# Thresholded attention and a leaky MLP on one core: q rows of two heads interleaved over the partitions, and the k and q loads placed earlier

## The chip, the cores and the metric

The kernel runs on one core of a Trainium2 chip. A core has TensorE (matrix products; in the profile PE for the products and PEld for the loads of their stationary operand, LDWEIGHTS), VectorE (DVE), ScalarE (ACT), GpSimd (POOL) and SyncE (SP), which run their own instruction streams and wait for each other on semaphores, and 16 DMA engines. The metric is device time in microseconds of one execution; smaller is better.

## The reference

Eight batches, eight heads, 576 tokens, head size 64. Attention keeps only scores within tau = 0.02 of their row's largest; then a two-layer MLP with a leaky ReLU runs over the concatenated heads.

```python
scores = scale * np.matmul(q, k.transpose(0, 1, 3, 2))          # scale = 1/8
thresh = np.max(scores, axis=-1, keepdims=True) - tau
scores = np.where(scores >= thresh, scores, -1e9)
scores = scores - np.max(scores, axis=-1, keepdims=True)
attn = np.exp(scores)
attn = attn / (np.sum(attn, axis=-1, keepdims=True) + 1e-09)
x = np.matmul(attn, v)                      # heads are then put side by side: (4608, 512)
h = x @ w_in                                # (512, 2048)
out = np.maximum(0.01 * h, h) @ w_out       # (2048, 512)
```

## The kernel before

**Steps.** The work is cut into 144 steps, 18 for each batch. The 576 rows of a batch are held as 64 partitions of nine consecutive tokens, so a block of 128 query rows is two of the nine token places t for 64 partitions each; the ninth place of two head pairs makes a block together. The heads are taken in four pairs p; a pair is the heads h = 0 and h = 1 of `(h f)`, that is f and f + 4. A step is one block of queries of one pair: two score tiles `sc[0]`, `sc[1]` of 128 queries x 576 keys. The steps of one block pair and one head pair (or, for the ninth place, two steps over all four pairs) make a unit; in the last batch some units are one step long.

**Number format.** q and k are float32. Each is split, scaled by 64, into a float16 high part and a float16 remainder (`hi` on ScalarE, L149; `x64` and `lo` on GpSimd, L153 and L159; in batch 0 `lo` on VectorE, L160). A score is the sum of three float16 products, high x high, high x low and low x high (`PRODS`).

**Halves and transposes.** A batch's q and k come in two halves hb, each with two head pairs g = 0, 1. `load_half` (L96) brings a half as a tile `km` or `qm` of 128 partitions, partition 64 f + p, where f is the pair within the half and p the row group. After the split, `ks` and `qs` hold (part, t, head, d) per partition. TensorE needs them with (head, d) on the partitions, so they are transposed. For k, one DMA transpose on SP (`turn`, L175) takes the whole 128-partition tile: 18 blocks of 128 x 128. For q, two DMA transposes (L179), one for each pair g, take 64 partitions each and write to `qst[:, g]`, so that the weights of a score product, `qt[r, g, qi, ds(2 * c, 2), :]`, are 128 neighbouring columns. In batch 0 alone TensorE does these transposes (`turn_pe`), and PSUM is copied out by ScalarE (L197) or VectorE (L199).

**One step.** Scores on TensorE (`scores`, L338, and L344 for the ninth place); eviction with row maximum on VectorE (`smax`, L398); the shift by maximum and tau, on ScalarE for one head (L524) and GpSimd for the other (L523, L525); one step later the clipping on VectorE (L554) and the exponentials with row sums on ScalarE (L559). Two steps after a unit's last step the reciprocals of its sums are put beside its weights in `w` (L542, L544), and a DMA transpose on SP turns `w` into `wt` (L548). Five steps after that, `LAG` = 7 after the last step, TensorE multiplies with v (`pv`, L369), VectorE scales into `xT` (L379, L385), and MLP units follow: `hp` and `op` products (L243), Relu on ScalarE (L257), the leak on VectorE (L223), eviction (L279), and the output's DMA on SP (L280).

**Order.** The program is laid out by hand in the loop over steps s, and every engine and queue runs its own instructions in that order. At the end of a step the functions listed for it in `ptick` and then `tick` are emitted. For half hb of batch b, with s0 = 18 (b - 1) and t0 = s0 + PREP[hb], PREP = (3, 9), (4, 9) for b = 1:

- k is loaded at step t0 - 4 and q at t0 - 3;
- `hi` of k runs on ScalarE at t0 - 1, of q at t0 + 1;
- `x64` and `lo` run on GpSimd at t0 to t0 + 6;
- k is transposed at t0 + 4, q's two pairs at t0 + 7 and t0 + 8.

So within a batch's 18 steps, the next batch's half 0 has `hi` at 2 and 4 and transposes at 7, 10 and 11; half 1 has `hi` at 8 and 10, transposes at 13, 16 and 17. The loads for half 1 stand at 5 and 6, those for half 0 at 17 of the batch before and 0. Weight transposes stand at the odd steps. All plain loads of q and k, all DMA transposes and all output stores are issued by SP, in order; v, w_in and w_out come by GpSimd's queue. `km`, `qm`, `ks` and `qs` have two buffers each, `kst` and `qst` four, `wt` four.

Of the kernel before, what the change touches and what calls it, by code (L numbers as in the profile page):

```python
# [10 lines left out]
FP16 = mybir.dt.float16  # L11
# [5 lines left out]
def kernel(  # L17
# [22 lines left out]
    nc = tc.nc  # L40
# [18 lines left out]
    ENDS = 130  # L59
    WOUT = 0  # L60
    SPOOL = 5

    sb = ctx.enter_context(tc.tile_pool(name="sb", bufs=1))
    ps = ctx.enter_context(tc.tile_pool(name="ps", bufs=1, space=bass.MemoryType.PSUM))
# [6 lines left out]
    if tau_f > 1.0:  # L71
# [10 lines left out]
        out=ident, in_=ident, compare_op=AX.is_equal, fill=0.0, base=0, pattern=[[-1, 128]], channel_multiplier=1)  # L82
# [6 lines left out]
    qms, kms, vts, qsts, ksts = {}, {}, {}, {}, {}  # L89
    qss, kss = {}, {}  # L90

    def load_half(src, store, nm, b, hb):


        m = store[b, hb] = sb.tile([128, 2, 576], FP32, tag=nm, bufs=2, name=nm)
        nc.sync.dma_start(  # L96
            out=m, in_=src[b, :, :, :].rearrange("(h f) (p t) d -> f p h (t d)", h=2, t=9)[
                ds(2 * hb, 2)].rearrange("f p h x -> (f p) h x"))

    anchor = [None]  # L100

# [25 lines left out]
    def split_tile(nm, b, hb):  # L127
        store = kss if nm == "k" else qss
        if (b, hb) not in store:
            store[b, hb] = sb.tile([128, 2, 9, 2, 64], FP16, tag=nm + "s", bufs=2, name=nm + "s")  # L130
        return store[b, hb]
# [31 lines left out]
    def turned(nm, b, hb):  # L163

        store = ksts if nm == "k" else qsts
        if (b, hb) not in store:
            shape = [128, 2, 9, 2, 64] if nm == "k" else [128, 2, 2, 9, 64]
            store[b, hb] = sb.tile(shape, FP16, tag=nm + "st", bufs=4, name=nm + "st")
        return store[b, hb]

    def turn(nm, b, hb, g=None):
        t = turned(nm, b, hb)
        s_ = split_tile(nm, b, hb)
        if nm == "k":
            nc.sync.dma_start(  # L175
                out=t.rearrange("p s t g r -> p (s t) (g r)"), in_=s_.rearrange("p s t h d -> p (s t h d)"),
                transpose=True)
        else:
            nc.sync.dma_start(  # L179
                out=t[:, g].rearrange("p s t r -> p (s t) r"),  # L180
                in_=s_[ds(64 * g, 64)].rearrange("p s t h d -> p (s t h d)"), transpose=True)

    def turn_pe(nm, b, hb, i, pieces, eng):

        t = turned(nm, b, hb)
        s_ = split_tile(nm, b, hb)
        for t0, n, tag, bufs, w in pieces:
            p_ = ps.tile([128, w, 128], FP16, tag=tag, bufs=bufs, name="tp")
            for j in range(n):
                nc.tensor.transpose(p_[:, j, :], s_[:, i, t0 + j, :, :].rearrange("p h d -> p (h d)"), ident)  # L190
            if nm == "k":
                src, dst = p_[:, 0:n, :], t[:, i, ds(t0, n), :, :].rearrange("p t g r -> p t (g r)")
            else:
                src = p_[:, 0:n, :].rearrange("p t (g r) -> p g t r", g=2)
                dst = t[:, :, i, ds(t0, n), :]
            if eng == "act":
                nc.scalar.activation(out=dst, in_=src, func=AF.Copy, bias=0.0, scale=1.0)  # L197
            else:
                nc.vector.tensor_copy(out=dst, in_=src)  # L199
# [125 lines left out]
    def scores(s, sc):  # L325

        b, c, p = steps[s]
        for t0, n in ((0, 5), (5, 4)):
            cols = ds(SC0 + 64 * t0, 64 * n)
            for i, (qi, ki) in enumerate(PRODS):  # L330
                for u in range(1 if c < 4 else 2):
                    hb, g = divmod(p + u, 2)
                    for h in range(2):
                        r = ds(64 * h, 64)
                        rhs = ksts[b, hb][r, ki, ds(t0, n), g, :]
                        qt = qsts[b, hb]
                        if c < 4:
                            nc.tensor.matmul(  # L338
                                out=sc[h][:, cols],
                                lhsT=qt[r, g, qi, ds(2 * c, 2), :].rearrange("p t r -> p (t r)"),  # L340
                                rhs=rhs, start=(i == 0), stop=(i == 2),
                                skip_group_check=True, tile_position=(64 * h, 0))
                        else:
                            nc.tensor.matmul(  # L344
                                out=sc[h][ds(64 * u, 64), cols], lhsT=qt[r, g, qi, 8, :],
                                rhs=rhs, start=(i == 0), stop=(i == 2),
                                skip_group_check=True, tile_position=(64 * h, 64 * u))

# [56 lines left out]
    def at(s, f, t=tick):  # L405
        t.setdefault(max(0, s), []).append(f)
# [55 lines left out]
    for b in range(1, B):  # L462
        s0 = 18 * (b - 1)
        for hb in range(2):
            t0 = s0 + (PREP1 if b < 2 else PREP)[hb]
            at(t0 - 4, lambda b=b, hb=hb: load_half(k, kms, "km", b, hb))
            at(t0 - 3, lambda b=b, hb=hb: load_half(q, qms, "qm", b, hb))
            at(t0 - 1, lambda b=b, hb=hb: hi("k", b, hb))
            at(t0 + 1, lambda b=b, hb=hb: hi("q", b, hb))

            for i, what in enumerate(("k0x", "k0l", "k1x q0x", "k1l", "q0l", "q1x", "q1l")):
                for w in what.split():
                    nm, h = w[0], int(w[1])
                    if w[2] == "x":
                        at(t0 + i, lambda nm=nm, h=h, b=b, hb=hb: after_anchor(x64(nm, b, hb, h)), ptick)
                    else:
                        for part in PARTS[nm]:
                            at(t0 + i, lambda nm=nm, h=h, b=b, hb=hb, part=part: after_anchor(lo(nm, b, hb, h, part)), ptick)
            at(t0 + 4, lambda b=b, hb=hb: turn("k", b, hb))
            for g in range(2):  # L480
                at(t0 + 7 + g, lambda b=b, hb=hb, g=g: turn("q", b, hb, g))
        for i in range(4):
            at(18 * b + i, lambda b=b, i=i: load_v(b, i))

# [12 lines left out]
    for s in range(NS + LAG + 1):  # L497
# [7 lines left out]
        while credit >= 1.0:  # L505
            f = next_o()
            if f:
                ou.append(f)
            f = next_h()
# [4 lines left out]
        if live:  # L514
            sc = [ps.tile([128, 1024], FP32, tag=f"sc{h}", bufs=1, name=f"sc{h}") for h in range(2)]
            scores(s, sc)
        last, prev = prev, None
        if live:
# [7 lines left out]
                out=P_[:, 0, :], in0=sa, scalar1=1.0, scalar2=bb[:, 0:1], op0=AX.mult, op1=AX.add)  # L526
            prev = (P_,) + unit_of[s]
        leak()
        for i in range(max(len(ou), len(hu))):
            o = ou[i]() if i < len(ou) else None  # L530
            h = hu[i]() if i < len(hu) else None
# [7 lines left out]
        if now is not None:  # L539
# [5 lines left out]
                out=W_[:, :, 1152:1280].rearrange("p i (h r) -> p i h r", h=2),  # L545
# [3 lines left out]
                out=uwt[now][:, 0:nw].rearrange("p i j r -> p (i j) r"), in_=W_.rearrange("p i c -> p (i c)"),  # L549
                transpose=True)  # L550
        if last is not None:
            P_, ui, i = last
# [22 lines left out]
    while hq or oq or leaky:  # L575
        for nx in (next_o, next_h):
            leak()
            f = nx()
            if f:
                f = f()  # L580
# [39 lines left out]
```

## Time and profile before

| | |
|---|---|
| median of 6 runs | 537.36 us (536.32 to 538.35) |
| the profiled execution | 536.81 us, of it 535.1 us from the first to the last instruction |
| granted TensorE clock, mean | 0.949 |
| DVE sf (L398), 288 | 746 ns each |
| LDWEIGHTS of scores, 64x128 (L338), 1536 | 97 ns each |
| score products of 320 columns, 768 | 313 ns each |
| LDWEIGHTS of v, 128x64 (L369), 1000 | 111 ns each |
| wt transposes on SP, 76 | 3.68 us median to issue, 6.1 us to land |
| kst transposes, 14 | 43.4 us of issue in all, 5.4 us to land |
| qst transposes, 28 | 41.8 us of issue in all, 4.3 us to land |
| km, qm loads, 16 each, 576 KB | 5.3 and 6.0 us to land |

How to read it: a page shows one execution. Busy time is per engine. A group of instructions is named by the line of the kernel, the engine, the operation and the tiles (out<-in). SPq is SP's queue of DMA issues: the time shown there is that of issuing, and the landing is told apart. The view of waits names the waiting engine and line, and what it waited for: microseconds in all, times, longest. In the timeline each line is a start and a length in microseconds, then the instruction; idle time before it stands in brackets. DMA share is the mean busy share of the 16 DMA engines; packets overlap, so that it can exceed 1. The chain of waits follows the work that ended last back through whatever released it.

### The profile page before, as it was taken

How to read it: one execution, taken by the hardware profiler on the slowest of the kernel's cores; microseconds unless marked ns; L12 is line 12 of the kernel's file. 1: busy time of each engine (PE TensorE's matmuls, PEld its weight loads, DVE VectorE, ACT ScalarE, POOL GpSimd, SP SyncE). 2: the span in 40 equal slices, each digit the busy share in tenths (PEclk: the TensorE clock that was granted, in tenths of full speed). 3: DMA queues.
4: the chain of work that ended last, by engine and by line, in shares of the span. 5: the costliest groups of instructions: out<-in, count | busy, mean ns of one | idle time of the engine just before them, and what ended most of it. 6: DMA issues, size and time to landing. Idle time of an engine off the chain costs nothing.

```text
span 535.1 us, 13446 instructions
## 1 busy us (share of the span) xinstructions
PE 476.2 (89%) x4912; PEld 294.3 (55%) x4912; DVE 463.2 (87%) x1213; ACT 421.5 (79%) x924; POOL 276.9 (52%) x476
## 2 busy tenths in 40 slices
PE   4657785999989997999989995999999998999996
PEld 3324453556555663666555663566655665566663
DVE  5976896999999996999998995899999999999542
ACT  6785885988799886898888985898799888688331
POOL 5475844675576645584566643575477643222000
PEclk9756897999999997999999998899999999999999
DMA  8999999999999999999999999999999999976401
GB/s 275 203 189 255 161 196 237 225 182 182 228 229 204 163 189 265 225 180 192 214 191 195 181 186 263 229 188 187 207 204 231 185 171 176 190 128 127 95 22 59
DMA packets 279617, 101.79 MB, mean 190 GB/s; under 512 B 254464, under 2 KB 266752, under 8 KB 279552
## 3 DMA queue, kind: packets, MB, share of 16 engines
q1 hardware_dynamic: 266496, 92.03, 90.6%
q0 software_dynamic: 13056, 8.92, 12.2%
q8 instruction: 38, 0.62, 0.5%
q14 instruction: 27, 0.22, 0.1%
HBM read 36.70 MB, written 9.44 MB: 86 GB/s over the span
## 4 chain that ended last, share of the span: by engine, by line
DVE 39%; PE 18%; issue 14%; DMA 13%; POOL 6%; ACT 6%; SPq 3%; POOLq 0%; DVEq 0%; ACTq 0%
DVE sf L398 15%; DMA km<-in_k_dram 8%; DVE gT L223 7%; DVE P L554 7%; PE op L243 6%; PE hp L243 5%; DMA wt<-w 4%; PE sc L338 4%; DVE w L544 4%; POOL P L525 3%; DVE osb L279 3%; DVE xT L379 2%; SPq L179 2%; PE pv L369 2%; ACT P L524 1%
## 5 line engine op out<-in xcount | busy, mean ns | idle before, releaser
L398 DVE TENSOR_SCALAR_CACHE_REDUCE sf<-sc 128x576 f32<-128x576 f32 x288 | 204.9, 746 | 9.9 <-PE sc L338 8.9
L559 ACT ACTIVATE w<-P 128x576 f16<-128x576 f16 x288 | 193.7, 674 | 8.1 <-DVE P L554 3.9
L243 PE MATMUL op<-wout,gT 128*128 128x512 f16 x576 | 151.0, 386 | 12.0 <-DVE osb L279 11.6
L243 PE MATMUL hp<-xT,win 128*128 128x256 f16 (+1 forms) x1344 | 153.9, 261 | 6.5 <-DVE gT L223 4.7
L338 PE MATMUL sc<-kst,qst 64*128 64x320 f16 (+1 forms) x1536 | 137.4, 298 | 19.4 <-DVE sf L398 18.7
L524 ACT ACTIVATE P<-sf,bb 128x576 f16<-128x576 f32 x144 | 111.1, 772 | 45.4 <-POOL bb L523 41.3
L243 PEld LDWEIGHTS <-win 128*128 128x128 f16 x1344 | 118.3, 99 | 51.1 <-issue 10.0
L223 DVE SCALAR_TENSOR_TENSOR gT<-hp,gT 128x512 f16<-128x512 f32 x144 | 98.2, 682 | 32.0 <-ACT gT L257 32.0
L338 PEld LDWEIGHTS <-qst 64*128 64x128 f16 x1536 | 76.2, 97 | 70.6 <-issue 51.9
L525 POOL TENSOR_SCALAR P<-sf,bb 128x576 f16<-128x576 f32 x139 | 104.8, 754 | 14.1
L257 ACT ACTIVATE gT<-hp 128x512 f16<-128x512 f32 x144 | 83.4, 579 | 18.9 <-PE hp L243 18.9
L243 PEld LDWEIGHTS <-gT 128*128 128x128 f16 x576 | 46.5, 98 | 75.2 <-issue 40.4
L523 POOL TENSOR_SCALAR bb<-mx 128x2 f32<-128x2 f32 x139 | 27.2, 196 | 109.5 <-DVE sf L398 99.4
L554 DVE TENSOR_SCALAR P<-P 128x1152 int16<-128x1152 int16 x144 | 81.5, 566 | 0.0
L369 PE MATMUL pv<-wt,v 128*64 128x256 f16 (+2 forms) x1000 | 55.7, 250 | 9.4 <-DMA wt<-w 9.3
L559 ACT ACTIVATION_READ_ACCUMULATOR w<-P 128x1 f32 x288 | 54.3, 188 | 0.0
L369 PEld LDWEIGHTS <-v 128*64 128x64 f16 x1000 | 37.4, 111 | 25.5 <-issue 22.2
L159 POOL TENSOR_TENSOR ks<-km,ks 128x320 f16<-128x320 f32 (+1 forms) x56 | 39.8, 730 | 11.4 <-DVE P L554 10.7
L149 ACT ACTIVATE ks<-km 128x640 f16<-128x640 f32 (+1 forms) x32 | 20.0, 672 | 30.6 <-DMA km<-in_k_dram 30.6
L159 POOL TENSOR_TENSOR qs<-qm,qs 128x576 f16<-128x576 f32 x28 | 35.8, 1279 | 14.2 <-DVE P L554 14.2
L544 DVE TENSOR_SCALAR w<-rc 128x256 f16<-128x256 f32 (+1 forms) x76 | 39.6, 521 | 2.6
L379 DVE TENSOR_TENSOR xT<-pv,wt 128x128 f16<-128x128 f32 x128 | 31.6, 289 | 5.9 <-PE pv L369 5.8
(35 smaller groups left out, 211.4 us busy)
## 6 DMA issues: line engine op xcount, KB each, us to landing
km<-in_k_dram SPq DMA_DIRECT2D x16, 576.0 KB, 5.3
qm<-in_q_dram SPq DMA_DIRECT2D x16, 576.0 KB, 6.0
out_dram<-osb SPq DMA_DIRECT2D x36, 256.0 KB, 3.7
v<-in_v_dram POOLq DMA_DIRECT2D x16, 160.0 KB, 5.6
v<-in_v_dram POOLq DMA_DIRECT2D x16, 128.0 KB, 5.8
win<-in_moe_w_in_dram POOLq DMA_DIRECT2D x8, 256.0 KB, 9.9
wout<-in_moe_w_out_dram POOLq DMA_DIRECT2D x8, 256.0 KB, 11.4
wt<-w SPq DMA_TRANSPOSE x76, 6.1
```

Source lines behind the costliest of these rows:

```text
L159: return nc.gpsimd.tensor_tensor(out=dst[:, h], in0=src[:, h], in1=h_[:, h], op=AX.subtract)
L223: nc.vector.scalar_tensor_tensor(out=G.g[u], in0=hp, scalar=0.01, in1=G.g[u], op0=AX.mult, op1=AX.add)
L243: nc.tensor.matmul(out=out_, lhsT=lhsT, rhs=rhs, start=start, stop=stop, skip_group_check=True)
L257: nc.scalar.activation(out=G.g[u], in_=hp, func=AF.Relu, bias=0.0, scale=0.99)
L338: nc.tensor.matmul(out=sc[h][:, cols], lhsT=qt[r, g, qi, ds(2 * c, 2), :].rearrange("p t r -> p (t r)"), rhs=rhs, start=(i == 0), stop=(i ...
L369: nc.tensor.matmul(out=o_[ds(64 * h, 64)], lhsT=vt[:, pp, h, j, :], rhs=w_[:, :, 4 * h + j, :], start=(j == 0), stop=(j == 4), skip_group_ ...
L398: nc.vector.tensor_scalar(out=sf, in0=sc[h][:, ds(SC0, 576)], scalar1=C, scalar2=None, op0=AX.mult, op1=AX.max, accum_out=mx[:, h : h + 1])
L524: nc.scalar.activation(out=P_[:, 1, :], in_=sB, func=AF.Identity, bias=bb[:, 1:2], scale=1.0)
L525: (nc.vector if s < SPOOL else nc.gpsimd).tensor_scalar(out=P_[:, 0, :], in0=sa, scalar1=1.0, scalar2=bb[:, 0:1], op0=AX.mult, op1=AX.add)
L544: nc.vector.tensor_scalar(out=W_[:, :, 1152:1280].rearrange("p i (h r) -> p i h r", h=2), in0=rc[:, 0:nw, :].unsqueeze(3).to_broadcast([12 ...
L554: anchor[0] = nc.vector.tensor_scalar(out=pi, in0=pi, scalar1=NEG, scalar2=None, op0=AX.max)
L559: nc.scalar.activation(out=uW[ui][:, i, ds(576 * h, 576)], in_=P_[:, h, :], func=AF.Exp, bias=exp_bias, scale=1.0, accum_out=usm[ui][:, i, ...
```

## The change

The q tile is loaded so that the two head pairs of a half take turns on the partitions: partition 2 p + f in place of 64 f + p. This takes two DMAs of 64 partitions each, every second one. `hi`, `x64` and `lo` are untouched, as they work on each partition alone. The transposed q tile then has the same shape as k's, with 128 columns for each part and token place in which the columns of pair g are every second one, and one DMA transpose of 128 partitions (at t0 + 7) stands in place of the two. The score products take their stationary operand at every second column, `[:, g::2]`. In batch 0 the copies out of PSUM write qst in the order in which it lies.

The loads of the next batch are placed by `LOADS = (-4, 3)`: for half 0, k at s0 - 4 and q at s0 - 3; for half 1, k at s0 + 3 and q at s0 + 4. For b = 1 the places of half 0 are below zero and become step 0. `hi`, `x64`, `lo` and the k transposes stay where they were.

```diff
@@ -59,6 +59,7 @@
     ENDS = 130
     WOUT = 0
     SPOOL = 5
+    LOADS = (-4, 3)
 
     sb = ctx.enter_context(tc.tile_pool(name="sb", bufs=1))
     ps = ctx.enter_context(tc.tile_pool(name="ps", bufs=1, space=bass.MemoryType.PSUM))
@@ -92,10 +93,14 @@
     def load_half(src, store, nm, b, hb):
 
 
+
         m = store[b, hb] = sb.tile([128, 2, 576], FP32, tag=nm, bufs=2, name=nm)
-        nc.sync.dma_start(
-            out=m, in_=src[b, :, :, :].rearrange("(h f) (p t) d -> f p h (t d)", h=2, t=9)[
-                ds(2 * hb, 2)].rearrange("f p h x -> (f p) h x"))
+        in_ = src[b, :, :, :].rearrange("(h f) (p t) d -> f p h (t d)", h=2, t=9)[ds(2 * hb, 2)]
+        if nm == "km":
+            nc.sync.dma_start(out=m, in_=in_.rearrange("f p h x -> (f p) h x"))
+        else:
+            for f in range(2):
+                nc.sync.dma_start(out=m.rearrange("(p f) h x -> f p h x", f=2)[f], in_=in_[f])
 
     anchor = [None]
 
@@ -164,21 +169,13 @@
 
         store = ksts if nm == "k" else qsts
         if (b, hb) not in store:
-            shape = [128, 2, 9, 2, 64] if nm == "k" else [128, 2, 2, 9, 64]
-            store[b, hb] = sb.tile(shape, FP16, tag=nm + "st", bufs=4, name=nm + "st")
+            store[b, hb] = sb.tile([128, 2, 9, 2, 64], FP16, tag=nm + "st", bufs=4, name=nm + "st")
         return store[b, hb]
 
-    def turn(nm, b, hb, g=None):
-        t = turned(nm, b, hb)
-        s_ = split_tile(nm, b, hb)
-        if nm == "k":
-            nc.sync.dma_start(
-                out=t.rearrange("p s t g r -> p (s t) (g r)"), in_=s_.rearrange("p s t h d -> p (s t h d)"),
-                transpose=True)
-        else:
-            nc.sync.dma_start(
-                out=t[:, g].rearrange("p s t r -> p (s t) r"),
-                in_=s_[ds(64 * g, 64)].rearrange("p s t h d -> p (s t h d)"), transpose=True)
+    def turn(nm, b, hb):
+        nc.sync.dma_start(
+            out=turned(nm, b, hb).rearrange("p s t g r -> p (s t) (g r)"),
+            in_=split_tile(nm, b, hb).rearrange("p s t h d -> p (s t h d)"), transpose=True)
 
     def turn_pe(nm, b, hb, i, pieces, eng):
 
@@ -188,11 +185,7 @@
             p_ = ps.tile([128, w, 128], FP16, tag=tag, bufs=bufs, name="tp")
             for j in range(n):
                 nc.tensor.transpose(p_[:, j, :], s_[:, i, t0 + j, :, :].rearrange("p h d -> p (h d)"), ident)
-            if nm == "k":
-                src, dst = p_[:, 0:n, :], t[:, i, ds(t0, n), :, :].rearrange("p t g r -> p t (g r)")
-            else:
-                src = p_[:, 0:n, :].rearrange("p t (g r) -> p g t r", g=2)
-                dst = t[:, :, i, ds(t0, n), :]
+            src, dst = p_[:, 0:n, :], t[:, i, ds(t0, n), :, :].rearrange("p t g r -> p t (g r)")
             if eng == "act":
                 nc.scalar.activation(out=dst, in_=src, func=AF.Copy, bias=0.0, scale=1.0)
             else:
@@ -337,12 +330,12 @@
                         if c < 4:
                             nc.tensor.matmul(
                                 out=sc[h][:, cols],
-                                lhsT=qt[r, g, qi, ds(2 * c, 2), :].rearrange("p t r -> p (t r)"),
+                                lhsT=qt[r, qi, ds(2 * c, 2)].rearrange("d t a b -> d (t a b)")[:, g::2],
                                 rhs=rhs, start=(i == 0), stop=(i == 2),
                                 skip_group_check=True, tile_position=(64 * h, 0))
                         else:
                             nc.tensor.matmul(
-                                out=sc[h][ds(64 * u, 64), cols], lhsT=qt[r, g, qi, 8, :],
+                                out=sc[h][ds(64 * u, 64), cols], lhsT=qt[r, qi, 8].rearrange("d a b -> d (a b)")[:, g::2],
                                 rhs=rhs, start=(i == 0), stop=(i == 2),
                                 skip_group_check=True, tile_position=(64 * h, 64 * u))
 
@@ -463,8 +456,8 @@
         s0 = 18 * (b - 1)
         for hb in range(2):
             t0 = s0 + (PREP1 if b < 2 else PREP)[hb]
-            at(t0 - 4, lambda b=b, hb=hb: load_half(k, kms, "km", b, hb))
-            at(t0 - 3, lambda b=b, hb=hb: load_half(q, qms, "qm", b, hb))
+            at(s0 + LOADS[hb], lambda b=b, hb=hb: load_half(k, kms, "km", b, hb))
+            at(s0 + LOADS[hb] + 1, lambda b=b, hb=hb: load_half(q, qms, "qm", b, hb))
             at(t0 - 1, lambda b=b, hb=hb: hi("k", b, hb))
             at(t0 + 1, lambda b=b, hb=hb: hi("q", b, hb))
 
@@ -477,8 +470,7 @@
                         for part in PARTS[nm]:
                             at(t0 + i, lambda nm=nm, h=h, b=b, hb=hb, part=part: after_anchor(lo(nm, b, hb, h, part)), ptick)
             at(t0 + 4, lambda b=b, hb=hb: turn("k", b, hb))
-            for g in range(2):
-                at(t0 + 7 + g, lambda b=b, hb=hb, g=g: turn("q", b, hb, g))
+            at(t0 + 7, lambda b=b, hb=hb: turn("q", b, hb))
         for i in range(4):
             at(18 * b + i, lambda b=b, i=i: load_v(b, i))
```

## The prediction

> **What bounds the kernel now.** I read the page first.
>
> ```profile
> PE 476.2 (89%) x4912; PEld 294.3 (55%) x4912; DVE 463.2 (87%) x1213; ACT 421.5 (79%) x924; POOL 276.9 (52%) x476
> DMA  8999999999999999999999999999999999976401
> ```
>
> TensorE and VectorE are busy for almost nine tenths, and so, in every slice up to the tail, are the DMA engines. Which of them sets the pace is read by stretch. The next view gives busy time from the first score eviction of one batch to that of the next, for batches 1 to 6 (first column: window; then its length, busy time of PE, PEld, DVE, ACT, POOL; the granted clock, the DMA share and GB/s).
>
> ```profile
> 70.40:132.10 61.70, 54.15 (x548) 32.71 (x547) 55.27 (x145) 50.13 (x113) 35.92 (x60) 0.94 1.09 205
> 132.10:189.70 57.60, 54.93 (x602) 34.84 (x601) 56.29 (x148) 51.27 (x115) 35.40 (x60) 1.00 1.13 208
> 189.70:251.80 62.10, 58.24 (x577) 35.00 (x576) 55.96 (x149) 51.36 (x115) 35.47 (x60) 0.95 1.09 207
> 251.80:311.00 59.20, 56.19 (x609) 35.29 (x608) 56.13 (x148) 51.17 (x115) 35.44 (x60) 1.00 1.16 195
> 311.00:374.80 63.80, 58.23 (x577) 35.11 (x576) 55.91 (x149) 51.37 (x115) 35.46 (x60) 0.95 1.13 211
> 374.80:432.50 57.70, 56.38 (x609) 35.47 (x608) 56.28 (x148) 51.26 (x115) 35.40 (x60) 1.00 1.13 207
> ```
>
> The six batches take 362.1 us, 60.35 each, and they alternate: a long one is followed by a short one. VectorE does the same 56 us of work in each. What the engines alone would need: in an undisturbed stretch the chain's sf pieces start at 289.46, 295.65, 301.96, 308.13 and 314.43, 6.24 us for two steps, and one pair of a batch takes 6.8 (404.18 to 410.99); 8 x 6.24 + 6.8 = 56.7 us. So 3.6 us of a batch is loss, 21.9 us over the six. The DMA share is above 1 throughout (packets overlap).
>
> Where the loss shows, from the view of waits:
>
> ```profile
> ACT ks L149 <- DMA km<-in_k_dram: 30.6, 9, 6.3
> PE pv L369 <- DMA wt<-w: 9.3, 5, 4.2
> ```
>
> ScalarE stands still for a k load, most often at step 2 of a batch's own count, and sometimes TensorE for a transposed weight tile. The timeline around 140 us shows why the load is late:
>
> ```profile
> 131.59 1.30 SPq L179 DMA_TRANSPOSE qst<-qs  x1
> 133.07 4.56 SPq L548 DMA_TRANSPOSE wt<-w  x1
> 137.68 1.34 SPq L179 DMA_TRANSPOSE qst<-qs  x1
> 139.07 1.33 SPq L96 DMA_DIRECT2D km<-in_k_dram  x1
> ...
> 141.77 13.77 SPq L548 DMA_TRANSPOSE wt<-w  x3
> 144.56 1.26 ACT L149 ACTIVATE ks<-km 128x640 f16<-128x640 f32 x2 [1.81 <-DMA km<-in_k_dram]
> ```
>
> SP issues without a pause, and behind its work: VectorE had finished the w of the weight transpose at 141.77 by 138.13. Read the same way, the same unit's transpose was 6.2 us late one batch on (195.75 to 201.90), then 2.8, 8.3 and 3.2. The long batches (stalled on k) let SP catch up; in the short ones it falls behind again, by 2.5, 5.5 and 3.4 us. So the in-order SP queue with the DMA engines behind it needs about 60 to 65 us a batch, more than the engines' 56.7: it is the bound in the middle, and the k stall is how that shows.
>
> What makes the queue slow:
>
> ```profile
> qm<-in_q_dram SPq DMA_DIRECT2D x16, 576.0 KB, 6.0
> wt<-w SPq DMA_TRANSPOSE x76, 6.1
> qst<-qs SPq DMA_TRANSPOSE x28, 4.3
> kst<-ks SPq DMA_TRANSPOSE x14, 5.4
> ```
>
> A k transpose of 128 partitions lands in 5.4 us; one of q, of 64 and so half the data, in 4.3. Two stretches with only transpose packets moving, the first a q transpose (issued 131.59), the second a weight transpose (133.07):
>
> ```profile
> 133.00:134.50 1.50, 1.50 (x22) 0.99 (x21) 1.50 (x4) 1.31 (x4) 0.77 (x2) 1.00 0.99 143
> 137.00:138.50 1.50, 1.50 (x16) 0.86 (x15) 1.47 (x5) 1.26 (x2) 0.88 (x2) 1.00 1.27 290
> ```
>
> The last column is the point: 143 GB/s against 290 with no other traffic beside either. The half-height transpose drains at half the rate.
>
> **The change part by part**, against the profiled execution's 536.8 us (span 535.1 and 1.7 around it); the median of six runs is 537.36, 0.6 above.
>
> (a) Two q transposes become one of 128 partitions, 14 times. Each half is 18 x 64 x 256 bytes = 295 KB, 2.06 us at 143 GB/s, 4.12 for two. The whole one is 590 KB: 2.03 us at 290 GB/s if the queue is backed up, 3.10 if it goes as kst's mean issue on SP (43.4 us for 14). Saved per pair 1.0 to 2.1 us; two pairs a batch, 2.0 to 4.2 us; I take the middle, 3.1. SP's own issue time stays: two at 1.49 (41.8 us over 28) against one at 3.10.
>
> (b) k and q loads move on SP: for half 0 of the next batch from steps 17 and 18 to 14 and 15, for half 1 from 5 and 6 to 3 and 4. k of half 0 is thereby issued ahead of one weight transpose (step 15), both q transposes (16, 17) and the weight transpose of 17: in the timeline from 139.07 to about 127, where the k transpose of step 13 ends (issued 123.26, 3.60 long). With 5.5 to 6.4 us to land it is there by about 133, and ScalarE asks at 142.7. For half 1 the lead grows from 9 to 15 us of program steps, against the worst seen, 8 us late plus 6.8 to land. So the k waits in the loop go: 5.7, 1.8, 4.5, 1.4, 6.3 and 1.9 us for half 0, 4.4 and 2.2 for half 1. That time is no gain by itself, since it is what let SP catch up. What is late next is the weight transpose: the one issued behind the moved loads is pushed back by their 0.6 + 2 x 0.47 us of issue and some 3.5 us of transfer (1.18 MB at the 330 GB/s of the load stretch, 142 to 147 us). Its multiplication comes 5 to 8 us after landing where SP keeps up (landed 126.97, used 133.53), 0.04 where it doesn't (446.23, 446.27). In return the weight transpose of step 1, the one with the smallest slack today, has two loads fewer ahead of it. Buffers don't hold the loads: km and qm have two, and the last reader of the earlier use (POOL's L159, step 15 at the latest for half 1, 9 for half 0) comes before both new places.
>
> (c) Each q load becomes two of 64 partitions, every second one: one more issue of 0.47 us, 16 times, 7.5 us of SP time. In the loop SP has that, as its long transposes (wt 3.7 median, 3.0 at best) wait on the drain and not on issue. At the start it lies on the chain (a qm piece from 1.32 us on, 4.91 long): +0.5. The Trainium skill, "DMA: Bandwidth & Descriptors", Rules for kernel authors, speaks against this part: two transfers over parts of the partitions serialize, and one of 128 should be used. Its figure of about 2 us fixed per DMA (Anatomy of one DMA, for the other kind of queue) would add, as an estimate by that page, 28 us over the 14 loop loads if none overlapped; km and qm landing 1.5 us apart here (86.57, 88.05) shows that they do overlap.
>
> (d) The score weights (L338, L344) are read at every second column. No strided weight load is in the trace. Nearest rows: 64x128 at 97 ns, 128x64 at 111 ns: 128 columns load faster than 64, so there is a fast way that a stride may lose. Bounds: 0, and 2 x 111 - 97 = 125 ns more per load. Loads of the two heads run in pairs (12 in 0.63 us beside 12 matmuls in 0.91), so six a step are serial: 0 to 0.75 us a step; a part hides behind matmuls of 120 ns. A gain is excluded, nothing gets narrower. I take 0, by the nearest row in shape (the same 64x128 load), and keep the other end as a rival. On this the skill's "TensorE: Matmul & The Clock Gate", Weight-path perf modes, says that the fast load holds for 128 weights in packed or strided columns up to a step of 1,024, but also that it reads 32 bits at a time, which at every second 16-bit column carries one weight in place of two; no run here shows which tells.
>
> (e) The PSUM copies of batch 0's q (L199, 752 ns) write runs in order; at most 0.3 us, taken as 0.
>
> Sum: a batch needs 60.35 - 3.1 = 57.25, just over the engines' 56.7; unevenness stays (the short batches hold about 0.9 over 56.7 with a small stall), of which I add 0.55: 57.8. Six batches: -15.3. Batch 0: its k wait of 4.36 us goes, but its weight transposes land only 1.1 us ahead (56.30, used 57.39), so half: -2. Batch 7: the pv waits at 446 and 454 come from the backlog, a step of 4.8 for 3.3: -1.5. Start +0.5. Together -18.3: 518.5 on the profiled execution's scale, 519 on the median's.
>
> **The rivals.**
> A, the forecast: 510 to 526. The low end is the whole loss gone (21.9 + 4.4 + 1.5 = 27.8: 509.6).
> B, the DMA queue stays the bound: the merged transpose saves only the 2.0, and the moved loads collide with the weight transposes of 13 to 17. The k wait turns into a pv wait. For it: the queue's need of 60 to 65 in the short batches; against it: 143 against 290. A batch of 59.4 gives -5.7, to about 531; the band is 526 to 535.
> C, slower: strided weight loads. TensorE is busy 54 to 58 us of a batch, so what isn't hidden comes straight on. With 66 ns exposed (half of the 125) a step takes 6 x 66 = 0.40 us more, a batch 56.7 + 7.1 = 63.8, six +21, batches 0 and 7 some +9: 567. The gain is gone from about 30 ns exposed a load (57.25 + 3.2 = 60.4).
> D, no change: the waits trade places exactly; 537.
>
> **How the numbers follow.** A 0.62, B 0.16, C 0.19, D 0.03. The point is A's, 519. The range 508 to 538 holds A, B and D; C lies above it. Faster by over 0.2% (about what a measurement of this kernel can tell from no change): A and B, 0.78; within: D, 0.03; slower: C, 0.19. A's own range is 510 to 526.
>
> **What would show it.** (a) qst lands in about 5.4 us, 14 of them, at 250 GB/s or more; DMA share falls. (b) ACT's wait for km in the loop falls below 5 us; batches of 57 to 58.5 us with no alternation. (c) qm x32 with 288 KB. (d) LDWEIGHTS <-qst stays within 5 ns of 97 and sc matmuls at 298. I am wrong by B if PE pv's wait for wt grows beyond 15 us, by C if the qst loads take over 120 ns.

## The result and the profile after

The changed kernel takes 533.37 us (median of 19 runs, 526.54 to 537.33) against 538.41 us for the kernel before, timed beside it: ratio 0.9884, 95% interval 0.9857 to 0.9910. It is faster, by 1.2%, where 3.4% was forecast (537.36 to 519). The ratio leaves out single runs that were slow throughout; by the medians of all runs the gain is 0.9%. The profiled execution of the changed kernel took 530.9 us.

The page of the changed kernel, in the rows that answer to those shown of before:

```profile
PE 474.7 (90%) x4912; PEld 294.3 (56%) x4912; DVE 463.8 (88%) x1213; ACT 424.2 (80%) x924; POOL 278.7 (53%) x476
DMA  8999999999999999999999999999999999966301
```

Work and DMA load look as before. The stretches from the first score eviction of one batch to the next, batches 1 to 6 (length second; at the end the granted TensorE clock, the DMA share and GB/s):

```profile
71.20:132.20 61.00, 54.59 (x548) 32.70 (x547) 55.23 (x145) 50.62 (x112) 36.02 (x60) 0.94 1.13 208
132.20:192.60 60.40, 56.17 (x603) 35.22 (x602) 56.80 (x148) 51.68 (x115) 35.50 (x60) 0.97 1.13 209
192.60:250.00 57.40, 55.64 (x578) 34.45 (x577) 55.85 (x149) 51.70 (x115) 35.56 (x60) 1.00 1.15 217
250.00:307.50 57.50, 55.85 (x610) 35.26 (x609) 56.51 (x149) 51.78 (x115) 35.52 (x60) 1.00 1.13 204
307.50:369.30 61.80, 57.11 (x578) 34.68 (x577) 55.71 (x150) 51.71 (x114) 35.85 (x60) 0.97 1.13 218
369.30:427.80 58.50, 55.90 (x610) 35.27 (x609) 56.57 (x149) 51.76 (x115) 35.49 (x60) 1.00 1.18 201
```

356.6 us in place of 362.1, and three batches of 60 to 62 remain. Two things stand in them. One is the granted clock: 0.94, 0.97 and 0.97 in these three, 1.00 in the others. Each of the three holds a stretch at half the clock (third number from the end):

```profile
83.50:90.30 6.80, 5.34 (x28) 2.61 (x30) 2.98 (x7) 2.75 (x8) 2.90 (x5) 0.50 1.40 199
155.20:158.60 3.40, 3.40 (x44) 1.76 (x39) 1.53 (x4) 0.56 (x2) 0.59 (x1) 0.50 1.06 267
325.80:329.20 3.40, 3.40 (x25) 1.65 (x22) 1.33 (x5) 0.94 (x1) 0.00 (x0) 0.50 1.23 265
```

TensorE had just stood still, or still did, for 3.9 us (to 84.96), 2.3 us (to 154.84) and 2.6 us (to 325.65), each time for a transposed tile. The kernel before has three such stretches of 6.8 us (from 88.1, 207.5 and 330.4), in its own three longest batches and beside standstills of 4.3, 3.7 and 5.4 us. As an estimate, half the clock costs at most half of these stretches, 6.8 us after and 10.2 before; no run takes this part from the waits that go with it. The other thing is the waits, by total:

```profile
PE pv L362 <- DMA wt<-w: 18.3, 9, 5.8
DVE xT L372 <- PE pv L362: 13.2, 8, 5.0
PEld L331 <- DMA qst<-qs: 7.2, 4, 4.2
ACT ks L154 <- DMA km<-in_k_dram: 5.3, 2, 3.0
```

ScalarE's wait for k went from 30.6 us to 5.3; in batches 1 to 6 alone from 23.8 to nothing. TensorE's wait for transposed weights went from 9.3 to 18.3 (in batches 1 to 6 from 1.4 to 10.7), VectorE waits behind it, and there is a new wait for the transposed q, all of it in batches 1 to 6. SP's queue around the load, the same place that the prediction showed of before:

```profile
127.25 0.58 SPq L100 DMA_DIRECT2D km<-in_k_dram  x1
...
128.69 4.57 SPq L540 DMA_TRANSPOSE wt<-w  x1
133.31 1.33 SPq L103 DMA_DIRECT2D qm<-in_q_dram  x2
134.75 5.09 SPq L176 DMA_TRANSPOSE qst<-qs  x1
140.01 3.64 SPq L540 DMA_TRANSPOSE wt<-w  x1
```

The k load is issued at 127.25, as forecast. The last line is the weight transpose of step 17. VectorE had its input ready at 131.95; it is issued 8.1 us later, lands at 146.63, and TensorE takes it at 146.67: no slack. Between the k load and the q load stands a weight transpose, and the merged q transpose takes 5.09 us to issue. The DMA issues (KB each, microseconds to landing), then four short stretches:

```profile
qm<-in_q_dram SPq DMA_DIRECT2D x32, 288.0 KB, 4.7
wt<-w SPq DMA_TRANSPOSE x76, 6.6
kst<-ks SPq DMA_TRANSPOSE x14, 5.5
qst<-qs SPq DMA_TRANSPOSE x14, 5.7
```

```profile
128.70:130.20 1.50, 1.50 (x26) 0.82 (x15) 1.15 (x4) 1.50 (x5) 0.18 (x1) 1.00 0.74 89
136.90:138.40 1.50, 1.50 (x17) 0.87 (x16) 1.47 (x6) 1.11 (x2) 0.94 (x2) 1.00 0.69 78
139.00:140.50 1.50, 1.50 (x19) 1.02 (x19) 1.50 (x6) 1.31 (x5) 0.88 (x3) 1.00 1.28 272
113.50:115.00 1.50, 1.50 (x12) 0.98 (x10) 1.50 (x5) 1.50 (x5) 0.91 (x3) 1.00 1.14 214
```

The third is the merged q transpose: 272 GB/s, against 143 for a half before. The fourth is the merged q transpose that SP issued at 111.83, with nothing else moving, and it gets 214. Transposes of 128 partitions are seen near 290 and near 215 GB/s, in the kernel before too (216 from 106.5 to 108, a k transpose). What decides between the two is not known.

The first stretch is the start of the k load behind transposes. The second is the end of the q load, before that q transpose gets going. In it few packets are SP's (q1), and most of the bytes are a v load of GpSimd's queue (q0; packets, MB, share of the 16 engines):

```profile
q0 software_dynamic: 124, 0.08, 62.0%
q1 hardware_dynamic: 17, 0.03, 5.3%
```

These two stretches take 1.5 us each at 78 to 89 GB/s, a third of the third stretch's rate, while SP has work queued. The changed kernel has three such groups of plain loads a batch (k of half 0; q of half 0; k and q of half 1), the kernel before two.

### The profile page after: what moved, and what is told of

It is laid out like the page before. It is cut to its first block, busy times and chain, and to the rows that moved or that the text cites. A ratio compares the mean times of both kernels' runs of the same rounds, so it can differ in the third digit from the quotient of the medians.

```text
span 529.2 us, 13454 instructions
## 1 busy us (share of the span) xinstructions
PE 474.7 (90%) x4912; PEld 294.3 (56%) x4912; DVE 463.8 (88%) x1213; ACT 424.2 (80%) x924; POOL 278.7 (53%) x476
## 4 chain that ended last, share of the span: by engine, by line
DVE 49%; DMA 16%; PE 14%; issue 12%; POOL 5%; ACT 3%; SPq 0%; POOLq 0%; DVEq 0%; ACTq 0%
DVE sf L391 20%; DMA wt<-w 13%; DVE gT L216 9%; DVE P L546 8%; PE op L236 5%; DVE w L536 5%; PE sc L331 3%; PE hp L236 3%; DVE osb L272 3%; DVE xT L372 3%; POOL P L517 2%; PE pv L362 2%; DMA qst<-qs 2%; ACT w L551 1%; POOL bb L515 1%
## 5 line engine op out<-in xcount | busy, mean ns | idle before, releaser
L236 PE MATMUL hp<-xT,win 128*128 128x256 f16 (+1 forms) x1344 | 150.7, 258 | 0.0
L517 POOL TENSOR_SCALAR P<-sf,bb 128x576 f16<-128x576 f32 x139 | 106.0, 763 | 14.3 <-POOL bb L515 0.4
L362 PE MATMUL pv<-wt,v 128*64 128x256 f16 (+2 forms) x1000 | 57.0, 254 | 19.2 <-DMA wt<-w 18.3
L362 PEld LDWEIGHTS <-v 128*64 128x64 f16 x1000 | 38.5, 113 | 35.8 <-issue 31.4
L126 POOL DMA_DIRECT2D v<-in_v_dram x32 | 20.5, 642 | 22.7 <-PE sc L331 10.1
## 6 DMA issues: line engine op xcount, KB each, us to landing
wout<-in_moe_w_out_dram POOLq DMA_DIRECT2D x8, 256.0 KB, 11.6
```

The lines of the kernel that those rows point to most:

```text
L236: nc.tensor.matmul(out=out_, lhsT=lhsT, rhs=rhs, start=start, stop=stop, skip_group_check=True)
L362: nc.tensor.matmul(out=o_[ds(64 * h, 64)], lhsT=vt[:, pp, h, j, :], rhs=w_[:, :, 4 * h + j, :], start=(j == 0), stop=(j == 4), skip_group_ ...
L517: (nc.vector if s < SPOOL else nc.gpsimd).tensor_scalar(out=P_[:, 0, :], in0=sa, scalar1=1.0, scalar2=bb[:, 0:1], op0=AX.mult, op1=AX.add)
```

## The experiments

Two readings stood at the start. P: the merged transpose relieves the DMA queue, and the new load places give a part back. M: the merge gives nothing, and the loads' new places are the whole gain.

**The two parts alone.** Merge alone, against the changed kernel:

```diff
-            at(s0 + LOADS[hb], lambda b=b, hb=hb: load_half(k, kms, "km", b, hb))
-            at(s0 + LOADS[hb] + 1, lambda b=b, hb=hb: load_half(q, qms, "qm", b, hb))
+            at(t0 - 4, lambda b=b, hb=hb: load_half(k, kms, "km", b, hb))
+            at(t0 - 3, lambda b=b, hb=hb: load_half(q, qms, "qm", b, hb))
```

> The changed kernel with the loads at their old places (k of half 0 at step 17 of the batch before, q at 0; half 1 at 5 and 6). Theory P (placement: the merged transpose relieves the DMA queue by about 1.8 us a pair, and the new load places give it back by delaying the weight transpose of step 17): the merge alone is worth more than the whole change, about 2% (526 against 538), with ACT waiting for km less than 30 us and PE pv for wt less than 10. Theory M (the merge gives nothing since the half-rate drain was covered by other waits, the whole gain is from the loads): within 0.3% of before, ACT still waits some 30 us for km.

Loads alone, against the kernel before:

```diff
+    LOADS = (-4, 3)
...
-            at(t0 - 4, lambda b=b, hb=hb: load_half(k, kms, "km", b, hb))
-            at(t0 - 3, lambda b=b, hb=hb: load_half(q, qms, "qm", b, hb))
+            at(s0 + LOADS[hb], lambda b=b, hb=hb: load_half(k, kms, "km", b, hb))
+            at(s0 + LOADS[hb] + 1, lambda b=b, hb=hb: load_half(q, qms, "qm", b, hb))
```

> The kernel before with the loads at the new places, two q transposes kept. Theory P: slower than before or equal (0 to +1%), the k waits gone and PE waiting for wt 20 us or more, as the queue's work is unchanged and the weight transpose of step 17 now stands behind the loads. Theory M: this alone gives the 1.2%.

Measured: merge alone 0.9784 (0.9725 to 0.9843), 529.32 us; loads alone 1.0011 (0.9974 to 1.0048). Theory M falls on both. The whole change gains 1.2%, its first half by itself 2.2%: the second half takes back about 1%. The waits of the kernel with the loads alone:

```profile
PE pv L370 <- DMA wt<-w: 21.6, 12, 4.4
...
ACT ks L150 <- DMA km<-in_k_dram: 3.8, 2, 2.5
```

ScalarE's 30.6 us of waiting are gone there too, TensorE's wait for weights has grown from 9.3 to 21.6 us, and nothing is won: the wait changed its place. The merge alone keeps its k wait (28.0 us in its profiled execution, one of 535.3 us) and has 11.8 us of waiting for wt, where P had said less than 10.

**Is the DMA queue the bound?** The changed kernel without its loop's q transposes; batches 1 to 7 use batch 0's transposed q, so their scores are not the reference's:

```diff
-            at(t0 + 7, lambda b=b, hb=hb: turn("q", b, hb))
+            qsts[b, hb] = qsts0[hb]
```

> The changed kernel without its 14 q transposes in the loop: batches 1 to 7 take batch 0's transposed q, so the scores of these batches are not those of the reference; loads, splits and all else stay. If the DMA queue sets the pace, 14 x 3 us less of it brings the batches to 57 to 58 us and the time to about 515. If the engines or the waits between them set it, under 5 us are gained (528 or more).

Measured: 0.9496 (0.9453 to 0.9539), 511.29 us. Four of its batches, by the same windows:

```profile
126.90:183.40 56.50, 54.89 (x603) 34.84 (x601) 56.19 (x148) 51.46 (x115) 35.40 (x60) 1.00 1.09 194
183.40:239.60 56.20, 56.07 (x577) 34.43 (x576) 55.61 (x149) 51.45 (x115) 35.46 (x60) 1.00 1.09 206
239.60:296.10 56.50, 56.07 (x609) 35.49 (x608) 56.19 (x148) 51.46 (x115) 35.41 (x60) 1.00 1.04 197
296.10:352.30 56.20, 56.07 (x578) 34.42 (x576) 55.61 (x149) 51.46 (x115) 35.46 (x60) 1.00 1.09 200
```

56.2 to 56.5 us, every batch alike: that is the engines' own time, put at 56.7 in the prediction, and it appears as soon as 14 transposes (49.4 us of issue in all in the changed kernel) are off the queue. The granted clock is 1.00 in each, so the half-clock stretches go with the waits. The queue is the bound.

**What do the new places cost?** First, k and q of half 0 side by side behind the weight transpose of step 15:

```diff
-    LOADS = (-4, 3)
+    LOADS = (-3, 3)
...
-            at(s0 + LOADS[hb] + 1, lambda b=b, hb=hb: load_half(q, qms, "qm", b, hb))
+            at(s0 + LOADS[hb] + hb, lambda b=b, hb=hb: load_half(q, qms, "qm", b, hb))
```

> The changed kernel with k and q of half 0 both at step 15, side by side in SP's order behind the weight transpose of that step, where they stood on either side of it. If what costs is the change between plain loads and transposes (each some 1 to 2 us of nearly empty DMA engines in the trace of after), one change fewer a batch gives 1 to 2 us each, 6 to 10 us in all (about 524). If it is only the amount of work ahead of the weight transpose of step 17, nothing changes (within 0.4% of the changed kernel).

Measured: 0.9791 (0.9753 to 0.9829), 527.67 us, clear of the changed kernel's interval. One group of loads in SP's queue, in its trace:

```profile
132.00:133.00 1.00, 1.00 (x13) 0.73 (x12) 1.00 (x5) 0.96 (x4) 0.08 (x1) 1.00 0.73 85
133.00:135.50 2.50, 2.50 (x29) 1.47 (x26) 2.50 (x8) 2.32 (x5) 1.41 (x3) 1.00 1.02 356
136.50:138.00 1.50, 1.50 (x15) 0.78 (x12) 1.47 (x5) 1.40 (x3) 0.75 (x1) 1.00 0.69 26
138.50:139.50 1.00, 1.00 (x15) 0.61 (x12) 1.00 (x3) 0.81 (x4) 0.40 (x2) 1.00 1.28 291
```

The group starts slowly (85 GB/s for 1 us), runs at 356, and ends with 1.5 us at 26 GB/s until its last stragglers are in; then transposes run at 291. The end has a rival, though. An instruction fetch of 16 KB begins between 135.5 and 136.5, and transposes slow down after such a fetch without any load: in the trace of before one begins between 134.5 and 135.5, and from 135.5 to 136.5 only transposes move, at 57 GB/s. So a group seems to have a price besides its bytes, and the trace alone doesn't say how much. From this came theory S (switch): each group of plain loads among the transposes costs, wherever it stands. Its rival J (jam): what counts is how much stands ahead of the weight transpose of step 17. Three kernels move the loads out of the dense steps 13 to 17, the second with one transpose between k and q again, the third with half 1 at its old places:

```diff
-    LOADS = (-4, 3)
+    LOADS = (-7, 3)
```

> The changed kernel with k and q of half 0 at steps 11 and 12: side by side in SP's order (no weight transpose at step 12) and ahead of the dense stretch of steps 13 to 17 (k transpose, two weight transposes, q transpose). Theory J (jam: what costs is the work that stands ahead of the weight transpose of step 17, which in the changed kernel is issued 4 to 9 us late): that transpose is on time again, better than the loads at step 15 (527.7), to 518 to 523. Theory S (switch: it costs each time plain loads and transposes change places on the DMA engines, whatever the step): as the loads at step 15, within 0.4%.

```diff
-    LOADS = (-4, 3)
+    LOADS = (-8, 3)
```

> The same one step earlier: k at step 10 behind the q transpose, q at step 11 behind the weight transpose of that step, so that one weight transpose stands between the two loads. Theory J: equal to the loads at 11 within 0.4%. Theory S: slower than the loads at 11 by the 5 to 6 us that lie between the changed kernel and the loads side by side at step 15.

```diff
-    LOADS = (-4, 3)
+    LOADS = (-7, 5)
```

> The loads of half 0 at 11 and 12 and those of half 1 back at 5 and 6, as in the kernel before. If the lead of half 1 matters (k waits of 4.4 and 2.2 us at step 8 in the kernel before), slower than with half 1 at 3 and 4 by 2 to 5 us; if the weight transposes of steps 1 and 3 gain from the later loads, faster by as much.

Measured: 0.9717 (0.9673 to 0.9760), 525.8 us; 0.9806 (0.9753 to 0.9860); 0.9758 (0.9709 to 0.9808). The split costs 0.9% (532.2 against 525.8 us; the intervals just touch) where in SP's order only the one weight transpose between k and q differs, as S has it. Leaving the dense stretch is worth some 0.7% (0.9717 against 0.9791, and the intervals overlap), and as much with the loads split (0.9806 against the change's 0.9884): more than the 0.4% that S allowed, and less than J promised. So both have a part. Half 1's lead is not resolved.

The q transpose of half 1 behind the weight transpose of step 17:

```diff
-            at(t0 + 7, lambda b=b, hb=hb: turn("q", b, hb))
+            at(t0 + 7 + hb, lambda b=b, hb=hb: turn("q", b, hb))
```

> The changed kernel with the merged q transpose of half 1 one step later, so that SP issues it behind the weight transpose of step 17 and not ahead of it. Theory J: PE's wait for wt falls from 18 us to under 8 and the time by some 4 us (about 529); but step 4 of the next batch needs this q, and PE's wait for qst, 6 to 7 us in the changed kernel, may grow to 15 and take it back. Theory S: no change (within 0.4% of the changed kernel), as the number of switches stays.

Measured: 1.0077 (1.0033 to 1.0121), nearly 2% slower than the changed kernel, so neither theory's number. Which wait took it is not known; that q then comes too late for step 4 is likely, not shown.

**Doses.** The number of groups of plain loads a batch, from one to four:

```diff
-    LOADS = (-4, 3)
+    LOADS = (-7, 3)
...
-            at(s0 + LOADS[hb] + 1, lambda b=b, hb=hb: load_half(q, qms, "qm", b, hb))
+            at(s0 + LOADS[hb] + 1 + hb, lambda b=b, hb=hb: load_half(q, qms, "qm", b, hb))
```

> Loads at 11 and 12 for half 0, and for half 1 k at 3 and q at 5, so that the weight transpose of step 5 stands between them: three clusters a batch. Theory S: about 1% slower than with two (ratio about 0.980). Theory J: the same amount of work ahead of every later transpose, so as with two clusters (0.972).

The same with `LOADS = (-8, 3)`:

> Both halves split: k at 10 and q at 11, k at 3 and q at 5, four clusters a batch. Theory S: about 2% slower than with two (ratio 0.990). Theory J: as with two or three.

The changed kernel again:

> The changed kernel itself, beside the others on one chip (three clusters a batch, one split by the weight transpose of step 15): ratio 0.988 as before. Theory S: equal to the other kernel with three clusters within 0.6%. Theory J: slower than it by 1% or more, since its loads stand in the dense stretch of steps 13 to 17.

And one group:

```diff
-    LOADS = (-4, 3)
+    LOADS = (-7, -7)
...
-        m = store[b, hb] = sb.tile([128, 2, 576], FP32, tag=nm, bufs=2, name=nm)
+        m = store[b, hb] = sb.tile([128, 2, 576], FP32, tag=nm, bufs=3, name=nm)
...
-                G.g[u] = sb.tile([128, nj, G.n], FP16, tag="gT", bufs=16, name="gT")
+                G.g[u] = sb.tile([128, nj, G.n], FP16, tag="gT", bufs=12, name="gT")
```

> All k and q loads of the next batch side by side at steps 11 and 12, one cluster of plain loads a batch in place of two (km and qm get three buffers, and gT 12 in place of 16 to make room). Theory S (each cluster of plain loads among the transposes costs the DMA engines about 1.6 us): one cluster fewer, about 1% below the two-cluster kernel with loads at 11 and 3, that is about 3.8% below before (ratio 0.962, 518). Theory J (amount of work ahead of a weight transpose): 2.4 MB in a row delay the weight transposes of steps 13 and 15 by 7 us, more than their slack in part, so slower than with two clusters (ratio 0.975 or more).

| groups a batch, merged transpose | ratio to before (95% interval) |
|---|---|
| 1: all at 11 | 0.9833 (0.9785 to 0.9881) |
| 2: half 0 at 11, half 1 at 3 | 0.9717 (0.9673 to 0.9760) |
| 2: 11 and 5 | 0.9758 (0.9709 to 0.9808) |
| 2: old places (merge alone) | 0.9784 (0.9725 to 0.9843) |
| 2: 15 and 3 | 0.9791 (0.9753 to 0.9829) |
| 3: 10 split, 3 | 0.9806 (0.9753 to 0.9860) |
| 3: 11, 3 split | 0.9865 (0.9815 to 0.9916) |
| 3: the change, twice | 0.9884 (0.9857 to 0.9910), 0.9878 (0.9841 to 0.9916) |
| 4: both split | 0.9922 (0.9883 to 0.9961) |

From two to four groups the means rise as theory S has it (0.976, 0.985, 0.992), by 0.7 to 0.9% a group, though kernels with the same number of groups lie up to 0.8% apart. The changed kernel is within 0.2% of the one with half 1's loads split (0.9865), where J had it slower by 1% or more. In that kernel, less stands ahead of the weight transpose of step 5 than with two groups, and it is still slower (0.9865 against 0.9717), also against J alone. As an estimate, 1% is 5 us over some six batches, so near 0.9 us a batch and group of time that isn't hidden. With one group S falls: 2.4 MB in a row make the weight transposes behind them late, and that kernel's TensorE waits 22.1 us for wt. There J holds: a group must not be longer than the slack of what stands behind it. (That kernel also has four gT buffers fewer, whose share wasn't measured.)

**Is the price one of order in SP's queue?** The loads of batches 1 to 7 through another queue, at the change's places, by ScalarE:

```diff
-            nc.sync.dma_start(out=m, in_=in_.rearrange("f p h x -> (f p) h x"))
+            (nc.sync if b == 0 else nc.scalar).dma_start(out=m, in_=in_.rearrange("f p h x -> (f p) h x"))
...
-                nc.sync.dma_start(out=m.rearrange("(p f) h x -> f p h x", f=2)[f], in_=in_[f])
+                (nc.sync if b == 0 else nc.scalar).dma_start(out=m.rearrange("(p f) h x -> f p h x", f=2)[f], in_=in_[f])
```

> The changed kernel with the k and q loads of batches 1 to 7 issued by ScalarE, so through another DMA queue, at the same steps (-4, 3). Theory S1 (what a cluster of loads costs is order: transposes behind loads in SP's one queue wait until the loads are done): transposes go on beside the loads, and the time falls to that of the kernel with two clusters or below it, 518 to 526 (ratio 0.960 to 0.975). Theory S2 (the engines themselves lose time when they mix the two kinds): 0.985 or more, whatever the queue; ScalarE's issue time (32 + 14 issues of some 0.5 us) comes on top.

By GpSimd (`nc.gpsimd` in place of `nc.scalar`, each behind the last clipping like the v loads):

> The same loads issued by GpSimd, through the queue of v. Theory S1: as from ScalarE or better, since GpSimd has idle time (53% busy), 0.960 to 0.975. Theory S2: 0.985 or more.

And the kernel before with its loads by ScalarE:

> The kernel before (two q transposes, old places) with the k and q loads of batches 1 to 7 issued by ScalarE. They no longer wait behind SP's backlog, so ACT's wait for km goes. Theory S1: faster than before by 1 to 2%, as the transposes no longer wait for loads. Theory S2 or a pure lack of DMA time: within 0.5% of before, the wait passing to PE pv for wt, as with the loads moved alone.

Measured: 1.0262 (1.0208 to 1.0316), 1.0719 (1.0638 to 1.0801) and 1.0482 (1.0426 to 1.0539). Theory S1, that the price is waiting in one queue, falls by a wide margin: free of SP's order, the loads cost more. The runs scatter (547 to 562 us, 572 to 622 and 553 to 569), but the fastest of each is slower than the median of before beside it, 537.75. S2 fits the first two; for the third it had said within 0.5% of before, and that is missed. The kernel before with ScalarE's loads, 8 us around a q load issued at 78.57:

```profile
83.50:91.50 8.00, 5.07 (x49) 3.12 (x45) 7.32 (x18) 7.94 (x18) 5.06 (x10) 1.00 1.48 108
```

SP's issues in that stretch:

```profile
77.11 5.19 SPq L548 DMA_TRANSPOSE wt<-w  x1
82.35 5.21 SPq L179 DMA_TRANSPOSE qst<-qs  x1
87.73 8.48 SPq L548 DMA_TRANSPOSE wt<-w  x1
```

The DMA engines are busy (share 1.48) and move 108 GB/s. The q transpose takes 5.21 us to issue, the longest of this run's 28 (median 1.41; before, 1.36), a weight transpose 8.48 (median 3.74). But it is not the k and q loads that run beside the transposes here. The queues in that stretch (packets, MB, share of the 16 engines; q1 is SP's, q0 GpSimd's, q10 ScalarE's):

```profile
q1 hardware_dynamic: 1931, 0.49, 101.9%
q0 software_dynamic: 517, 0.28, 41.7%
q10 hardware_dynamic: 36, 0.08, 3.1%
```

The k and q loads are nearly through, and the transposes run beside v loads, which GpSimd issues in every kernel here. In the 3.5 us ahead (80 to 83.5), where the k and q loads do move beside transposes, the engines reach 284 GB/s. The stretch is an extreme, too: from 75 to 135 us the share is 1.21 at 193 GB/s, against 1.09 to 1.16 at 195 to 211 in the batches of before. So the trace shows transposes and plain loads of another queue losing time together, with v's loads; that the k and q loads do the same to the transposes (theory S2 as it was meant) is argued, not shown. What the runs do show is that the transposes come later: TensorE's wait for wt is 38.8 us with ScalarE's loads in the kernel before (9.3 without) and 49.4 us with GpSimd's in the changed one (18.3). A rival is the time that issuing takes from ScalarE: 10.9 us in all in the kernel before, too little for its loss of 4.8%, but 25.3 us in the changed kernel, which could hold its loss. What happens inside the DMA engines is not settled by these runs.

## Why the prediction was right and wrong

**The bound: right.** The prediction read the in-order SP queue and the DMA engines behind it as the bound in the middle. The kernel without q transposes shows it, with the engines' own time within 0.5 us a batch of the forecast 56.7. What the reading left out is that the long batches are also the ones with a stretch at half clock.

**Step (a), the merge: right in its cause, put too high in size.** 143 GB/s became 272 in the one stretch and 214 in the other; 14 transposes land in 5.7 us (5.4 forecast) and take 49.4 us to issue (43.4 forecast). By itself it gives 2.2%, 11.6 us of 538.8. Spread over six batches that is 1.9 us each, the low end of the forecast's 2.0 to 4.2 and not the 3.1 that went into the sum. The rate of 290 was read from one stretch; at 215 GB/s a whole transpose takes 2.7 us and not 2.03. The DMA share did not fall (1.13 to 1.18 after, 1.09 to 1.16 before). With two groups of loads out of the dense stretch the best version gives 2.8%, some 15 us of 540.0, against 18.3 forecast.

**Step (b), the moved loads: this is the step that failed.** The k waits went as forecast (none left in batches 1 to 6; of the 5.3 us, 2.3 are at the start and 3.0 in batch 0), as did the reading that this is no gain by itself (loads alone: 1.0011). The prediction named the weight transpose as late next, and priced what stands ahead of it as 1.5 us of issue and 3.5 us of transfer, made good by what step 1's transpose gains. It left out that k at step 14 and q at 15 no longer stand side by side: the weight transpose of 15 comes between, and a third group of plain loads a batch has a price of its own, about 1% of the time (0.9884 against 0.9791 with the two side by side). Its beginnings could have been seen in the trace of before, where half 1's load starts at 109 GB/s (156.8 to 157.8); I took the rate of a load's middle (330 GB/s). It also has no term for a wait for the transposed q, which came to 7.2 us.

The profiled execution missed 518.5 by 12.4 us: 9.8 in batches 1 to 6 (356.6 against 6 x 57.8), 2.4 in batch 0, 0.3 in batch 7. Of the 9.8, some 5 are the third group's price, and some 4 more may be that of the dense stretch (0.7%, not resolved). The term for unevenness, 0.55 us a batch, was also put too small: three batches still take 60.4 to 61.8, and they are the ones with the half-clock stretches. These overlap with the prices above, and how much falls to each is open.

**Step (c), two q loads: small, as forecast.** The first score eviction comes 0.4 us later (12.5 to 12.9 us). With the two halves in it the merge alone still gains 2.2%, so the rule of the Trainium skill, "DMA: Bandwidth & Descriptors", Rules for kernel authors, against two transfers over parts of the partitions didn't decide here; no run has the merge without them.

**Step (d), strided weights: right.** The row of after:

```profile
L331 PEld LDWEIGHTS <-qst 64*128 64x128 f16 x1536 | 75.5, 98 | 74.3 <-issue 48.4 <-DMA qst<-qs 7.2 <-DVE qst L192 0.2
```

98 ns against 97: every second column costs nothing. Rival C is out. This agrees with the Trainium skill's "TensorE: Matmul & The Clock Gate", Weight-path perf modes, which lets the fast load have spaced columns; that it reads 32 bits at a time has no visible price here.

**Batches 0 and 7.** Batch 0 gained nothing (57.9 to 58.3 us, -2 forecast): its k wait shrank only from 4.4 to 3.0 us, and its wait for a weight transpose grew from 4.2 to 5.8. Batch 7 gained 1.2 us (1.5 forecast).

**The rivals.** The outcome is rival B (526 to 535): TensorE's wait for weights passed the 15 us named as its sign. Its first ground, a merge worth only 2.0 us a batch, is near the 1.9 measured. Its second, the moved loads colliding with the transposes of 13 to 17, was near the cause, but the larger share is the third group (0.9%); leaving that stretch is worth 0.7 to 0.8%, and not resolved. The range of 508 to 538 holds 533.4; the likeliest case and its band of 510 to 526 do not.

## What to carry to other kernels

Where a queue of DMA transposes sets the pace, take work off the queue before moving waits about: an earlier load only shifted the wait from one engine to another, and half-height transposes cost nearly the time of whole ones. Look at the granted clock of each stretch before putting a long batch down to waits alone. Keep plain loads together in the same queue as the transposes, in as few groups as the slack of what follows allows: here two groups of 1.2 MB a batch, and the loads at steps 11 and 12 beat both kernels (0.9717, 525.8 us). Don't send them through another engine's queue to get them out of the way before measuring that.

## What the runs showed of the hardware that was not expected

A transpose of 64 partitions drained at 143 GB/s, those of 128 at 214 to 216 or at 272 to 291, from the same queue. DMA transposes beside plain loads of another queue slowed down: 108 GB/s at a busy share of 1.48 over 8 us, beside GpSimd's v loads. With the k and q loads issued by ScalarE or GpSimd the kernel was 2.6 to 7.2% slower than before. After an instruction fetch transposes came at 57 GB/s for a microsecond with nothing else moving. TensorE's clock was halved for 3.4 or 6.8 us at each of six standstills of 2.3 to 5.4 us in batches 1 to 6 of the two traces. A stationary operand read at every second 16-bit column loads in 98 ns, as fast as a packed one (97).
